# A Fourier mixing layer and a SiLU feed-forward on one core: preparation of the operands cut into smaller pieces and reordered

## The chip, the cores and the metric

The kernel runs on one core of a Trainium2 chip. A core has five engines that work side by side, each with a queue of its own: TensorE (PE; its weight loads are shown as PEld), VectorE (DVE), ScalarE (ACT), GpSimd (POOL) and SyncE (SP), which here only issues DMAs. The metric is the device time of one execution in microseconds, as the median of several runs; less is better. The kernel before takes 760.5 us (median of three, 759.12 to 760.71).

## What is computed

With x of 2048 tokens by 512 features:

```python
a = x_ln @ hid_re.T ;  b = x_ln @ hid_im.T          # x_ln = layernorm(x)
h = x + (seq_re @ a - seq_im @ b)                   # sequence DFT, 2048 x 2048
out = h + silu(layernorm(h) @ w1) @ w2              # w1 512 x 1792, w2 1792 x 512
```

All data are fp32. The layernorms have no gain or bias.

## The kernel before, in words

**Arithmetic.** Every fp32 operand of TensorE is kept as two rounded parts: `hi`, a copy rounded to the format fp32r that ACT makes (`ph`, `X`, `S`, `T..h`, `wah`, `wsh`), and `lo`, the remainder, which DVE makes by a subtraction (`pl`, `wal`, `wsl`). One product is three matmuls (`three`, lines 106 to 108): hi by hi, weight hi by lo, weight lo by hi. Each matmul is 128 x 128 by 128 x 512.

**Stages**, in the order of TensorE:
- *plain(0,0)*, the plain stage: the real sequence DFT of half of the output tokens, in 16 steps of 24 matmuls. A step is named (jj, k, tau): jj is one of four tiles of 512 rows of x, k one of its halves of 256 rows (each holds two pieces a of 128 rows), tau one of two blocks of output tokens. A step needs the normalised x of (jj, k) as weights (`X`, hi and lo) and a chunk of the DFT matrix (`raw`, split into `ph` and `pl`). Two steps, tau 0 and 1, use the same X.
- *fast(1,0)*, then mix(0), fast(0,1), fast(1,1) and mix(1). The fast stages do other parts of the sequence DFT with seven products instead of eight (Strassen's scheme in Winograd's form); they need sums and differences of the quarters of x (`S` 1 to 4 for each jj), which `sums_x` makes. A fast stage has 28 steps of 12 matmuls: three groups of four (products 1, 3, 2), and then products 5, 7, 6, 4 for each jj, whose DFT operands are differences that DVE makes first (line 326). mix is the hidden DFT with the residual.
- `norm_h(q, tau, start)` is the second layernorm, spread over the time from `start` on: mean (+0: DVE sums, then a reduction over partitions on GpSimd), center (+7 and +9: DVE, and squares on ACT), variance (+12), root (+28) and scaling (+42, +44).
- *up(0)*, down(0), up(1), down(1): the feed-forward. up runs seven products per p (p = 0 to 6), each of 6 matmuls, in the same scheme; `prep_w1` makes the weights: `wah`/`wal` are the split of w1's quarters, `s1` to `s4` their sums, `wsh`/`wsl` the split of these. After product 1, 6 and 5 ACT copies the accumulator out (`cp`, `cp`, `cq`); after 2, 5 and 4 DVE adds such a copy (line 558), and ACT applies SiLU (line 554). Product 3 accumulates onto the same bank after product 5, so it needs the copy `cq` to be done.

**What sets the order.** The author writes an order by hand. A clock counts planned time: `step(n, ...)` lets n matmuls take n x 0.2265 us, so a step of 24 is 5.44 us and one of 12 is 2.72. Every piece of work is an event with a planned time: a step's `before` list gives leads ahead of its start (`PREP_US` 8, `LOAD_US` 18), its `after` list delays after its end, and `at(t, f)` an absolute time. The events are sorted by that time, and on DVE, ACT and GpSimd the instructions of a later event are issued behind those of an earlier one. Planned times are thus only an order: an engine never waits for the clock, but each of these three queues is worked off in order, and an instruction that waits holds up all that is behind it. Within one event, and on TensorE and SP, a scheduler of the language chooses the order.

**Memory.** Nearly every operand lives in one of 51 slots of 4 KB per partition (the pool `pages`). A load waits until its slot is free. PSUM has four tiles of two banks.

**x's normalisation before.** `norm_x` (line 135) does it all in one event: statistics of each tile of 128 rows (lines 142 and 143), a reciprocal square root by three Newton iterations of three small DVE instructions each (`rsqrt`, lines 91 to 102), the normalised copy `xc` on ACT (line 150) and X's hi part (line 163); the remainders follow in a later event (`rest`, line 169). For jj = 1, 2, 3 all four tiles are in one event, 15 us ahead of the step (jj, 0, 0), and its remainders 11 us ahead. For jj = 0 the first two tiles are done singly at the very start, 128 rows each, and the other two 11 us ahead of (0, 1, 0). `sums_x(jj)` comes right after step (jj, 1, 0) for every jj, its remainders 3 us later.

Of the kernel before, what the change touches and what calls it, by code (L numbers as in the profile page):

```python
# [7 lines left out]
F32 = mybir.dt.float32  # L8
# [7 lines left out]
P = 128  # L16
# [21 lines left out]
def fnet_ffn_kernel(  # L38
# [52 lines left out]
    def rsqrt(v, t, r, q):  # L91
# [6 lines left out]
        for a, b in ((r, q), (q, r), (r, q)):  # L98
            nc.vector.tensor_tensor(t, a, a, op=ALU.mult)
            nc.vector.tensor_tensor(t, t, v, op=ALU.mult)  # L100
            nc.vector.scalar_tensor_tensor(b, t, 1.5, a, op0=ALU.add, op1=ALU.mult)
# [33 lines left out]
    def norm_x(jj, which):  # L135

        n = len(which)
        mv = small.tile([P, 4, 2], F32, name="mv1")
        w = small.tile([P, 5, 4], F32, name="rs1")
        for j, (k, a) in enumerate(which):  # L140
            st = small.tile([P, 6], F32, name="st1")
            nc.vector.bn_stats(st, xraw[jj, k][:, a, :])
            nc.vector.bn_aggr(mv[:, j, :], st)
# [3 lines left out]
        for j, (k, a) in enumerate(which):  # L147
            if (jj, k) not in xc:
                xc[jj, k] = page(f"xc{jj}{k}")
            nc.scalar.activation(  # L150
                xc[jj, k][:, a, :], xraw[jj, k][:, a, :], AF.Identity, bias=w[:, 4, j : j + 1], scale=r[:, j : j + 1]
            )
# [59 lines left out]
    def begin(key):  # L212

        t = raw[key] = page("raw")
        part[key] = page("ph", F32R), page("pl", F32R)
        src = seq[0, 0, 0].rearrange("p (a t) -> p a t", a=2)
        for a in range(2):
            load_x(0, 0, slice(a, a + 1))
            nc.sync.dma_start(t[:, a, :], src[:, a, :])

    def begin_norm(key, a):
        hi, lo = part[key]
        nc.scalar.activation(hi[:, a, :], raw[key][:, a, :], AF.Copy)
        late["x", a] = [(lo[:, a, :], raw[key][:, a, :], hi[:, a, :])] + norm_x(0, [(0, a)])
        if a == 1:
            raw.pop(key)

    def plain(c, q):

        for jj, k, tau in ((jj, k, tau) for jj in range(NJ) for k in range(2) for tau in range(2)):  # L230
            key = ("A", c, q, jj, k, tau)

            def mm(jj=jj, k=k, tau=tau, key=key):
                hi, lo = part.pop(key)
                for i in range(2):
                    if jj == 0 and k == 0:
                        acc[c, q, i, tau] = banks(f"c{c}{q}{i}{tau}")
                for a in range(2):
                    for i in range(2):
                        w = X[i, k, jj]  # L240
                        for m in range(2):
                            d = slice(m * P, (m + 1) * P)
                            three(acc[c, q, i, tau][:, m, :], w[:, 0, a, d], w[:, 1, a, d], hi[:, a, :], lo[:, a, :],
                                  jj == 0 and k == 0 and a == 0, jj == NJ - 1 and k == 1 and a == 1)

            before, after = [], []
            if (jj, k, tau) == (0, 0, 0):
                before = [(99.0, lambda key=key: begin(key))]
                for a in range(2):
                    before += [(98.0 - a, lambda a=a, key=key: begin_norm(key, a)),  # L250
                               (97.5 - a, lambda a=a: rest(late.pop(("x", a))))]
            else:
                before = [(LOAD_US, lambda jj=jj, k=k, tau=tau, key=key: load_seq(c, q, jj, k, tau, key)),
                          (PREP_US, lambda key=key: prep_raw(key))]
            if (jj, k, tau) == (0, 1, 0):
                before = [(40.0, lambda: load_x(0, 1)), (PREP_US + 3, lambda: early("x0", lambda: norm_x(0, [(1, 0), (1, 1)]))),
                          (PREP_US + 1, lambda: rest(late.pop("x0")))] + before
# [453 lines left out]
```

## Time and profile before

| | us |
|---|---|
| median of the runs | 760.5 |
| the profiled execution, its time | 761.24 |
| its span, first to last instruction | 759.3 |
| PE busy | 717.4 (94%) |
| DVE busy | 496.4 (65%) |
| ACT busy | 313.5 (41%) |
| POOL busy | 49.9 (7%) |

The mean granted clock of TensorE is 0.986. The program has 3036 matmuls of the kernel's own, and 15 that only warm the array up at the start (line 664). Matmuls are pipelined: a matmul's listed time (0.39 us) is longer than the distance between two starts, so progress is read from starts, and a busy PE is not a PE at its peak. A bracket behind a row, as in `[2.33 <-ACT X L163]`, is the idle time of that engine ahead of the row and what ended it. A name such as `ph` in a row stands for all buffers of that name.

### The profile page before, as it was taken

The page shows a single profiled execution, that of the slowest core. Times are in us where ns is not written, and L with a number is a line of the kernel's source. Part 1 is how long each engine was busy: PE and PEld are TensorE (multiplying, and loading weights), DVE is VectorE, ACT ScalarE, POOL GpSimd, SP SyncE. Part 2 cuts the span into 40 slices and gives each one's busy share as a digit, 9 for nine tenths or more (in the row PEclk, how much of TensorE's full clock was granted, in tenths as well). Part 3 has the DMA queues.
Part 4 walks back from the last instruction along what each step waited for, and adds up shares of the span by engine and source line. Part 5 has one row for each costly group of instructions (what it writes and reads, how often), then busy time and mean ns, then how long its engine had stood idle before and what let it go on. Part 6 is the DMA issues. An engine that isn't in the chain of part 4 may idle for free. (4 is left out here: it accounts for less than half of the span.)

```text
span 759.3 us, 8093 instructions
## 1 busy us (share of the span) xinstructions
PE 717.4 (94%) x3051; PEld 573.0 (75%) x3051; DVE 496.4 (65%) x672; ACT 313.5 (41%) x389; POOL 49.9 (7%) x48
## 2 busy tenths in 40 slices
PE   7699899999999999989999989999999989999997
PEld 4487688888888888868888866768778766778885
DVE  6586666694845899778986955437879844449002
ACT  3525455444223445144443435545432345457000
POOL 0000000000002210130000000002510000000000
PEclk9999999999999999999999999999999999999999
DMA  9322338555366658486952220232420411043003
GB/s 340 131 110 83 140 102 315 156 208 190 139 246 226 222 196 311 172 333 230 319 213 83 84 83 28 83 111 81 170 56 30 149 53 48 29 133 116 1 0 111
DMA packets 39592, 110.66 MB, mean 146 GB/s; under 512 B 4097, under 2 KB 7681, under 8 KB 39553
## 3 DMA queue, kind: packets, MB, share of 16 engines
q1 hardware_dynamic: 35968, 98.58, 37.1%
q0 software_dynamic: 3584, 11.56, 4.1%
q8 instruction: 24, 0.39, 0.2%
q14 instruction: 16, 0.12, 0.1%
HBM read 95.43 MB, written 14.70 MB: 145 GB/s over the span
## 5 line engine op out<-in xcount | busy, mean ns | idle before, releaser
L80 DVE TENSOR_TENSOR pl<-raw,ph 128x1024 fp32r<-128x1024 f32 x51 | 67.0, 1342 | 64.8 <-ACT ph L76 58.8
L106 PE MATMUL c<-ph,X 128*128 128x512 f32 x128 | 51.7, 411 | 14.5 <-ACT ph L76 9.9
L76 ACT ACTIVATE ph<-raw 128x1024 fp32r<-128x1024 f32 x51 | 51.2, 1050 | 21.2 <-PE y L107 12.0
L326 DVE TENSOR_TENSOR raw<-raw,raw 128x1024 f32<-128x1024 f32 x48 | 58.7, 1222 | 0.0
L107 PE MATMUL c<-pl,X 128*128 128x512 f32 x128 | 51.6, 404 | 0.6 <-DVE pl L80 0.5
L554 ACT ACTIVATE g<-g 128x512 f32<-128x512 f32 x42 | 26.5, 630 | 61.6 <-DVE g L558 61.6
L108 PE MATMUL c<-ph,X 128*128 128x512 f32 x128 | 51.0, 400 | 0.0
L106 PEld LDWEIGHTS c<-ph,X 128*128 128x128 f32 x128 | 24.5, 194 | 22.9 <-ACT ph L76 12.6
L629 DVE TENSOR_TENSOR ho<-o,ho 128x512 f32<-128x512 f32 x16 | 10.0, 688 | 47.5 <-PE o L108 47.3
L80 DVE TENSOR_TENSOR pl<-g,ph 128x1024 fp32r<-128x1024 f32 x28 | 34.0, 1238 | 5.4 <-ACT ph L76 5.4
L108 PE MATMUL m<-ph,X 128*128 128x512 f32 x96 | 37.4, 389 | 0.0
L107 PE MATMUL m<-pl,X 128*128 128x512 f32 x96 | 37.4, 389 | 0.0
L106 PE MATMUL m<-ph,X 128*128 128x512 f32 x96 | 37.3, 389 | 0.0
L558 DVE TENSOR_TENSOR g<-yx,cp 128x512 f32<-128x512 f32 x14 | 9.7, 692 | 32.4 <-PE yx L108 32.4
L107 PEld LDWEIGHTS c<-pl,X 128*128 128x128 f32 x128 | 25.0, 195 | 7.2 <-DVE pl L80 1.7
L108 PEld LDWEIGHTS c<-ph,X 128*128 128x128 f32 x128 | 25.0, 195 | 5.4 <-DVE X L169 0.2
L76 ACT ACTIVATE ph<-g 128x1024 fp32r<-128x1024 f32 x28 | 28.4, 1044 | 0.0
L558 DVE TENSOR_TENSOR g<-v,cq 128x512 f32<-128x512 f32 x14 | 9.7, 691 | 26.0 <-ACT cq L573 24.4
L528 DVE TENSOR_TENSOR wal<-w,wah 128x768 fp32r<-128x768 f32 x14 | 13.4, 957 | 20.3 <-ACT wah L523 20.3
L150 ACT ACTIVATE xc<-x,rs 128x512 f32<-128x512 f32 x16 | 11.9, 805 | 35.3 <-DVE rs L146 26.0
L459 ACT ACTIVATE sq<-hr 128x1024 f32<-128x1024 f32 x8 | 8.5, 1062 | 36.9 <-DVE hr L455 23.1
L436 POOL PARTITION_ALL_REDUCE m<-m x4 | 15.1, 3764 | 126.1 <-DVE g L558 75.8
(330 smaller groups left out, 1998.3 us busy)
## 6 DMA issues: line engine op xcount, KB each, us to landing
raw<-in_seq SPq DMA_DIRECT2D x99, 512.0 KB, 4.5
w<-in_ffn SPq DMA_DIRECT2D x28, 256.0 KB, 2.9
w<-in_ffn SPq DMA_DIRECT2D x14, 512.0 KB, 3.7
hid<-in_hid SPq DMA_DIRECT2D x8, 512.0 KB, 4.3
c<-cd SPq DMA_DIRECT2D x8, 512.0 KB, 4.3
h<-in_xT SPq DMA_DIRECT2D x8, 512.0 KB, 5.0
hd<-h POOLq DMA_DIRECT2D x8, 512.0 KB, 3.2
hr<-hd SPq DMA_DIRECT2D x8, 512.0 KB, 3.9
```

Of the source, the lines that this page charges most:

```text
L76: nc.scalar.activation(hi, src, AF.Copy, scale=sign)
L80: nc.vector.tensor_tensor(lo, src, hi, op=ALU.subtract)
L106: nc.tensor.matmul(acc, wh, mh, start=first, stop=False, skip_group_check=on)
L107: nc.tensor.matmul(acc, wh, ml, start=False, stop=False, skip_group_check=on)
L108: nc.tensor.matmul(acc, wl, mh, start=False, stop=last, skip_group_check=on)
L150: nc.scalar.activation(xc[jj, k][:, a, :], xraw[jj, k][:, a, :], AF.Identity, bias=w[:, 4, j : j + 1], scale=r[:, j : j + 1])
L326: nc.vector.tensor_tensor(o, a, b, op=ALU.subtract)
L436: nc.gpsimd.partition_all_reduce(t[:, 1, :], t[:, 0, :], channels=P, reduce_op=REDUCE_ADD)
L528: nc.vector.tensor_tensor(al[:, 1:, :], r[:, 1:, :], ah[:, 1:, :], op=ALU.subtract)
L554: nc.scalar.activation(g[q, f][:, tau, :], src, AF.Silu)
L558: nc.vector.tensor_tensor(d, src, other, op=ALU.add)
L629: nc.vector.tensor_tensor(t[:, tau, :], a[:, tau, :], t[:, tau, :], op=ALU.add)
```

## The change

Six things, each an edit of the event lists but for the first:
- In `rsqrt`, where the operand has one column, the first two instructions of an iteration become one (a x v x a, with v as a scalar per partition).
- `norm_x` is cut into `stats_x`, `roots_x` and `norm_x`. For jj = 1, 2, 3 the two halves k get statistics, normalised copies and remainders of their own, with one root in between. For jj = 2 and 3 they lie 19 and 16 us (statistics), 15 (root), 11 and 10 (copies), 8 and 5 us (remainders) ahead of the step (jj, 0, 0), for jj = 1 everything but the loads 5 us later; x is loaded 28 and 27 us ahead instead of 24. For the second half of jj = 0 statistics and root lie 9 us ahead of step (0, 1, 0), the copies 6 and the remainders 4.
- The first two steps are turned round: 24 matmuls with the first 128 rows of x for both blocks of tokens, then 24 with the second 128 rows. Both blocks' chunks of the DFT matrix are loaded and split by halves.
- `sums_x` of jj = 2 and 3 moves out of the plain stage into fast(1,0): 1 us and 8 us after its start, the remainders 4 us after each.
- norm_h(0,1) starts 8 us after the beginning of fast(1,1) instead of 1 us.
- In up, a weight's preparation is three events instead of two: the hi copy and the four sums 11 us ahead, the sums' hi copy and the first remainder 9.6, the sums' remainder 8.2 (before: all but the last at 10, the last at 8). SiLU after products 2, 5 and 4 becomes an event of its own, 1.5 us behind the add.

The diff's core:

```diff
@@ rsqrt
-            nc.vector.tensor_tensor(t, a, a, op=ALU.mult)
-            nc.vector.tensor_tensor(t, t, v, op=ALU.mult)
+            if a.shape[-1] == 1:
+                nc.vector.scalar_tensor_tensor(t, a, v, a, op0=ALU.mult, op1=ALU.mult)
+            else:
+                nc.vector.tensor_tensor(t, a, a, op=ALU.mult)
+                nc.vector.tensor_tensor(t, t, v, op=ALU.mult)
@@ x's normalisation
+    def stats_x(jj, which):
+        if jj not in stats:
+            stats[jj] = [], small.tile([P, 4, 2], F32, name="mv1"), small.tile([P, 5, 4], F32, name="rs1")
+        done, mv, _ = stats[jj]
+        for k, a in which:
             st = small.tile([P, 6], F32, name="st1")
             nc.vector.bn_stats(st, xraw[jj, k][:, a, :])
+            nc.vector.bn_aggr(mv[:, len(done), :], st)
+            done.append((k, a))
+    def roots_x(jj):
...
+        return {t: (w[:, 4, j : j + 1], r[:, j : j + 1]) for j, t in enumerate(done)}
+    def norm_x(jj, which, factors):
...
@@ plain
+        keys = [("A", c, q, 0, 0, tau) for tau in range(2)]
+        at(-99, lambda: begin(keys))
+        for a in range(2):
+            at(-98 + 4 * a, lambda a=a: begin_x(keys[0], a))
+            at(-97 + 4 * a, lambda a=a: rest(late.pop(("x", a))))
+            at(-96 + 4 * a, lambda a=a: rest(begin_half(keys[1], a)))
+            step(24, lambda a=a: [mul(0, 0, tau, [a], part[key]) for tau, key in enumerate(keys)])
+        at(-40, lambda: load_x(0, 1))
+        at(clock[0] - 9, lambda: (stats_x(0, [(1, 0), (1, 1)]), early("r0", lambda: roots_x(0))))
+        at(clock[0] - 6, lambda: early("x0", lambda: norm_x(0, [(1, 0), (1, 1)], late.pop("r0"))))
+        at(clock[0] - 4, lambda: rest(late.pop("x0")))
...
+            if k == 0 and tau == 0:
+                for k2, l1, l2, l3 in ((0, 19, 11, 8), (1, 16, 10, 5)):
+                    tiles = [(k2, 0), (k2, 1)]
+                    l1, l2, l3 = (l - 5 * (jj == 1) for l in (l1, l2, l3))
+                    before += [(28 - k2, lambda jj=jj, k=k2: load_x(jj, k)),
+                               (l1, lambda jj=jj, tiles=tiles: stats_x(jj, tiles)),
+                               (l2, lambda jj=jj, tiles=tiles, k=k2:
+                                early(("x", jj, k), lambda: norm_x(jj, tiles, late["r", jj]))),
+                               (l3, lambda jj=jj, k=k2: rest(late.pop(("x", jj, k))))]
+                before.append((15 - 5 * (jj == 1), lambda jj=jj: early(("r", jj), lambda: roots_x(jj))))
-            if k == 1 and tau == 0:
+            if k == 1 and tau == 0 and jj < 2:
                 after += [(0, lambda jj=jj: early(("s", jj), lambda: sums_x(jj))),
                           (3, lambda jj=jj: rest(late.pop(("s", jj))))]
...
+        for jj in range(2, NJ):
+            t = clock[0] + 1 + 7 * (jj - 2)
+            at(t, lambda jj=jj: early(("s", jj), lambda: sums_x(jj)))
+            at(t + 4, lambda jj=jj: rest(late.pop(("s", jj))))
@@ up
-        nc.vector.tensor_tensor(al[:, 1:, :], r[:, 1:, :], ah[:, 1:, :], op=ALU.subtract)
-        nc.scalar.activation(sh, t, AF.Copy)
-        late["w", q, p] = [(sl, t, sh)]
+        late["w", q, p] = [[(al[:, 1:, :], r[:, 1:, :], ah[:, 1:, :])], [(sl, t, sh)]]
...
         def add(f, tau, src, other):
-            d = g[q, f][:, tau, :]
-            nc.vector.tensor_tensor(d, src, other, op=ALU.add)
-            silu(f, tau, d)
+            nc.vector.tensor_tensor(g[q, f][:, tau, :], src, other, op=ALU.add)
...
-                before = [(LOAD_US, lambda p=p: load_w1(q, p)), (PREP_US + 2, lambda p=p: prep_w1(q, p)),
-                          (PREP_US, lambda p=p: rest(late.pop(("w", q, p))))]
-            step(6, lambda n=n, p=p: mm(n, p), before, [(0, lambda n=n, p=p: post(n, p))])
+                def sums(p=p):
+                    _, [(_, t, sh)] = late["w", q, p]
+                    nc.scalar.activation(sh, t, AF.Copy)
+                    rest(late["w", q, p][0])
+                before = [(LOAD_US, lambda p=p: load_w1(q, p)), (PREP_US + 3, lambda p=p: prep_w1(q, p)),
+                          (PREP_US + 1.6, sums), (PREP_US + 0.2, lambda p=p: rest(late.pop(("w", q, p))[1]))]
+            after = [(0, lambda n=n, p=p: post(n, p))]
+            if n in (2, 5, 4):
+                f, tau = {2: (2 * p, 0), 5: (2 * p + 1, 1), 4: (2 * p + 1, 0)}[n]
+                after.append((1.5, lambda f=f, tau=tau: silu(f, tau, g[q, f][:, tau, :])))
+            step(6, lambda n=n, p=p: mm(n, p), before, after)
@@ order of the stages
-    norm_h(0, 1, clock[0] + 1)
+    norm_h(0, 1, clock[0] + 8)
```

More of the change, by code (lines that the diff above doesn't have):

```diff
@@ new lines, in mul @@
+        def mul(jj, k, tau, tiles, parts):
+            hi, lo = parts
+            if jj == 0 and k == 0 and 0 in tiles:
+                for i in range(2):
+                    acc[c, q, i, tau] = banks(f"c{c}{q}{i}{tau}")
+            for a in tiles:
+                for i in range(2):
+                    w = X[i, k, jj]
+                    for m in range(2):
+                        d = slice(m * P, (m + 1) * P)
+                        three(acc[c, q, i, tau][:, m, :], w[:, 0, a, d], w[:, 1, a, d], hi[:, a, :], lo[:, a, :],
+                              jj == 0 and k == 0 and a == 0, jj == NJ - 1 and k == 1 and a == 1)
```

73 lines of the change are left out of this document (23 added, 50 removed).

## The prediction, made before the changed kernel was run

> **What bounds the kernel now.** I read the windows by stage first, cut at the stages' first matmuls (columns: window, length, then busy time and instruction count of PE, PEld, DVE, ACT, POOL, the granted clock, DMA share, GB/s).
>
> ```profile
> 8.09:114.83 106.74, 93.78 (x384) 73.91 (x385) 70.94 (x167) 49.26 (x70) 1.23 (x2) 0.95 0.40 146
> 114.83:190.99 76.16, 76.16 (x338) 63.06 (x337) 53.48 (x48) 35.97 (x39) 1.06 (x2) 1.00 0.60 211
> 310.66:392.93 82.27, 79.19 (x337) 63.97 (x336) 72.00 (x76) 36.58 (x39) 12.68 (x11) 0.98 0.74 272
> 436.22:516.75 80.53, 73.43 (x295) 54.68 (x294) 38.80 (x58) 38.38 (x60) 1.06 (x2) 0.98 0.22 75
> 516.75:596.26 79.51, 76.83 (x337) 62.90 (x336) 66.50 (x91) 35.04 (x37) 18.55 (x12) 1.00 0.25 78
> 596.26:677.45 81.19, 73.49 (x295) 54.59 (x294) 38.86 (x62) 36.46 (x59) 0.00 (x0) 0.98 0.25 81
> 677.45:753.64 76.19, 76.19 (x338) 63.06 (x336) 25.64 (x26) 19.62 (x22) 0.00 (x0) 1.00 0.17 54
> ```
>
> TensorE is the bound. The second row is a stage without a gap: its 336 matmuls (28 steps of 12) in 76.16 us are 0.2267 us each. At that pace the plain stage (first row, 384) would take 87.0 us; it takes 106.7, a loss of 19.7. The third row, fast(1,1), loses 6.1; the two up stages (294 matmuls, 66.65 us) lose 13.9 and 14.5; down(0) loses 3.3. Only those losses can be won, and the waits of PE name them (waiter, releaser: total us, times, longest):
>
> ```profile
> PE c L106 <- ACT ph L76: 9.9, 5, 6.0
> PE yx L106 <- ACT cq L573: 9.7, 10, 2.0
> PE c L106 <- ACT X L163: 4.5, 2, 2.3
> PE yx L106 <- DVE g L558: 1.7, 10, 0.2
> ```
>
> Three of the four rows are waits that the change is aimed at: both c rows lie in the plain stage, the cq row in the up stages. The fourth stays.
>
> **Plain stage, what costs now.** The stalls on PE's timeline (start, length, then in brackets the idle time before it):
>
> ```profile
> 13.51 0.50 PE L106 MATMUL c<-ph,X 128*128 128x512 f32 x1 [2.33 <-ACT X L163]
> 14.42 0.63 PE L106 MATMUL c<-ph,X 128*128 128x512 f32 x1
> 17.73 0.39 PE L108 MATMUL c<-ph,X 128*128 128x512 f32 x1
> 23.70 0.73 PE L106 MATMUL c<-ph,X 128*128 128x512 f32 x2
> 36.27 1.22 PE L106 MATMUL c<-ph,X 128*128 128x512 f32 x2 [6.03 <-ACT ph L76]
> 87.14 0.74 PE L106 MATMUL c<-ph,X 128*128 128x512 f32 x2 [2.82 <-ACT ph L76]
> ```
>
> From 14.42 to 17.73 nine matmuls start, eight intervals of 0.41 instead of 0.23: a slow clock after the 2.33 us gap, 1.5 us more. A wait of 2 us therefore costs its length, some 0.3 of refilling, and perhaps 1.5. The 2.82 us gap at 87.14 brought no such stretch, so the length alone does not decide.
>
> The Trainium skill (TensorE: Matmul & The Clock Gate, Part 1) has the clock fall after at least one idle window of about 3.4 us, and advises against idle gaps over some 3 us. The row at 13.51 contradicts it: 2.33 us was enough here. By the page, the 2.1 us gap that I leave below would cost no 1.5, and the total would come out 1.5 lower.
>
> **Part by part.** Prices, from groups of the first 116 us (busy, mean ns | idle):
>
> ```profile
> L80 DVE TENSOR_TENSOR pl<-raw,ph 128x1024 fp32r<-128x1024 f32 x18 | 21.8, 1224 | 30.6 <-ACT ph L76 24.6 <-DMA raw<-in_seq 6.0
> L76 ACT ACTIVATE ph<-raw 128x1024 fp32r<-128x1024 f32 x18 | 17.9, 1043 | 0.0
> L150 ACT ACTIVATE xc<-x,rs 128x512 f32<-128x512 f32 x16 | 11.9, 805 | 35.3 <-DVE rs L146 26.0 <-issue 9.3
> L142 DVE BATCH_NORM_STATS2 st<-x 128x6 f32<-128x512 f32 x16 | 10.5, 676 | 2.2 <-DMA x<-in_x 2.2
> L169 DVE TENSOR_TENSOR S<-s,S 128x512 fp32r<-128x512 f32 x16 | 10.0, 685 | 0.0
> L163 ACT ACTIVATE X<-xc 128x512 fp32r<-128x512 f32 x14 | 7.7, 615 | 0.0
> L100 DVE TENSOR_TENSOR rs<-rs 128x1 f32<-128x1 f32 x6 | 1.0, 160 | 0.2
> ```
>
> *The fused root.* Only the two one-column roots of the first tile lose three instructions each, 0.16 busy and about 0.2 with the gap between dependent ones: 0.6 us ahead of the first matmul: it starts at 7.5, not 8.09. The fused form (a per-partition scalar operand) has no row; between 0.16 us as its neighbours and twice that, I take 0.16 (at twice, 0.5 less is won).
>
> *Two blocks on the first tile.* Half 0 now feeds 24 matmuls (to 13.2) before half 1 is needed. Half 1 adds the second block's two ops in front (ACT hi and DVE lo, 0.6 each), then its own chain, 0.6 shorter: its first X is there at 13.1. The 13.51 gap and its slow stretch go. These 48 matmuls end at 18.6, where before the next step began at 23.70. The new load of the second block's halves delays the x half behind it by 256 KB; it is needed only at 8.9, so nothing.
>
> *What is late next* is X of x rows (0,1). DVE runs the second block's lo until 14.6, then two statistics, the unfused two-column root (13 small ops) until 18.5, ACT two xc and one X: PE starts at 20.75. Gap 2.1 us, with refill 2.5, and I charge the slow clock, 1.5.
>
> *Pieces.* Before, four tiles of statistics, root, four xc and four X ran as one block and the step's ph stood behind them in ACT's queue:
>
> ```profile
> 30.07 0.16 DVE L146 SCALAR_TENSOR_TENSOR rs<-mv,rs 128x4 f32<-128x4 f32 x1
> 30.27 2.92 ACT L150 ACTIVATE xc<-x,rs 128x512 f32<-128x512 f32 x4 [6.62 <-DVE rs L146]
> 33.10 2.17 ACT L163 ACTIVATE X<-xc 128x512 fp32r<-128x512 f32 x4
> 35.17 1.99 ACT L76 ACTIVATE ph<-raw 128x1024 fp32r<-128x1024 f32 x2
> ```
>
> Now ph of that step (1,0,0) is queued ahead of the xc. I laid the queues in the new order with the prices above (ends, us). DVE: X's remainders 22.1, first statistics 23.5, pl of (0,1,1) 24.7, second statistics 26.1, root 28.7, pl of (1,0,0) 29.8, four sums 32.2, X's remainders 33.4. ACT: ph of (0,1,1) 22.4, of (1,0,0) 23.4, two xc 30.3, X 31.0 and 31.5, S 33.6, second piece 36.2, ph of (1,0,1) 37.2. PE: (0,1,0) from 20.75, 24 matmuls and 0.3 for a late remainder, (0,1,1) from 26.5, ready for (1,0,0) at 31.95 (before: 36.27), when its X has been there since 31.0. The two later tiles go the same way. Left over are X's remainder behind the four sums (0.6), ph and pl of (1,0,1) behind S's and the second piece (0.4), pl of (1,1,0) behind the next statistics (0.9), (2,0,0) 1.0, (2,0,1) 0.7, (3,0,0) 0.8; with 0.2 at the very start and 4.0 above the new loss is 8.6 instead of 19.7. With the 0.6 of the start: **11.7 us** won. Bounds: 17 (all gone but the first gap), 5 (half of the old big gaps kept). x's earlier loads (28 against 24 us) run on SP far ahead of use and cost nothing while slots of the pool are free.
>
> *Sums of tiles 2 and 3 moved* behind the plain stage, into fast(1,0), which has no loss now.
>
> ```profile
> 103.34 0.69 DVE L176 TENSOR_TENSOR s<-xc,xc 128x512 f32<-128x512 f32 x1
> 116.17 3.89 ACT L76 ACTIVATE ph<-raw 128x1024 fp32r<-128x1024 f32 x4
> ```
>
> Per tile it is four sums, four S, four remainders: 2.5 us of DVE, 3.5 from first sum to last S, 2.5 of DVE. The second row shows that ACT comes back to ph only 1.3 us after fast(1,0) begins at 114.83, once C is copied out. From there I lay both queues: pl of the fourth step at +2.4, sums of tile 2 to +6.1, remainders to +11.7, sums of tile 3 from +12.8; ph of the seventh step stands behind their S until +17.35, its pl ends at +18.6, and PE wants it at +16.5 (six steps of 2.72, one matmul). **2.2 us lost.** Bounds: 0 (the queues had 1 us in hand twice) to 5.
>
> *norm_h(0,1) seven us later.* It touches fast(1,1):
>
> ```profile
> 319.68 4.40 DVE L80 TENSOR_TENSOR pl<-raw,ph 128x1024 fp32r<-128x1024 f32 x2
> 320.02 3.98 POOL L436 PARTITION_ALL_REDUCE m<-m  x1 [37.17 <-DMA raw<-in_seq]
> 325.41 1.06 ACT L459 ACTIVATE sq<-hr 128x1024 f32<-128x1024 f32 x1 [10.76 <-DVE hr L455]
> ```
>
> While GpSimd reduces, two pl take 4.4 us instead of 2.4, and ACT stands 10.8 us before the squares, with every ph of this stage behind them: that is the whole 6.1. Seven us later in the order DVE has worked off its backlog from the stage before, the mean starts at about 320.1 and three more ph/pl pairs precede center, so the steps up to 337 are covered. Then the variance (1.9 us on DVE), its reduction (another 2 of slowing) and, in ACT's queue, t5h ahead of the twelfth step's ph: pl is ready at 343.5, wanted at 340.85; with refill 3.1 is lost. POOL's stores of C come ahead of the reduction and gain time; what needs the normalised h (its loads, 40 us before up(0)) has over 20 us in hand. **3.0 us won**; bounds 6.1 and 0, below nothing if the root and the scalings, now deeper in the stage where DVE needs 2.3 of each 2.7 us, wait once more (-2).
>
> *Up stages.* One period, at T3's wait for the copy cq (PE's rows last: T7's final matmul, T3's first):
>
> ```profile
> 458.75 0.83 ACT L523 ACTIVATE wah<-w 128x768 fp32r<-128x768 f32 x1
> 460.95 1.06 ACT L529 ACTIVATE wsh<-ws 128x1024 fp32r<-128x1024 f32 x1 [1.36 <-DVE ws L527]
> 461.92 0.58 ACT L573 ACTIVATE cq<-yx 128x512 f32<-128x512 f32 x1
> 461.48 0.39 PE L108 MATMUL v<-T7h,wsl 128*128 128x512 f32 x1
> 462.55 0.50 PE L106 MATMUL yx<-T3h,wsh 128*128 128x512 f32 x1 [0.68 <-ACT cq L573]
> ```
>
> cq stands behind wsh, which waits 1.36 us for the fourth sum, which DVE does after wal, which waits for wah. The change puts wal behind the sums and wsh into a later piece: the order on ACT becomes wah, SiLU, wsh, cq, with the sums done under wah. In my layout cq ends 0.5 us before T7 does, so T3 waits no more: from start to start 1.07 instead of 0.23, 0.84, in four periods of each up stage. The first wait of each (2.0, the longest in the waits) shrinks by 1.4 and loses its slow stretch (1.5). That is 6.3 per stage, **12.6 us** in two. The SiLUs 1.5 us later delay only their own outputs, needed in down, 9 us or more on; the wait for the add (1.7 us) stays, and so do T5's and down's first. Bounds: 16 (the add's waits, 1.7 and as much refill, go too) and 0 (another order of the products on PE, which this kernel does not write out by hand, puts cq behind something else).
>
> **The sum.** 11.7 - 2.2 + 3.0 + 12.6 = 25.1. The profiled execution took 761.24 (span 759.3), so 736.1; it stands 0.7 above the median of 760.5.
>
> **Rivals.**
> 1. *Up keeps its wait* (PE's order shifts, or the SiLU ahead of wsh waits for its add and hands its lateness on to cq). For it: cq now has one more instruction ahead, and that add needs T4's end. Against: T4 ends four products before. 736.1 + 12.6 = 748.7.
> 2. *DVE stays late in the plain stage.* Its work there is only redistributed, and 70.9 busy of 106.7 us becomes some 61 of 95 (two tiles' sums gone). If every new piece still meets its step late, half of the gain is left: 736.1 + 5.9 = 742.0.
> 3. *All new waits miss.* No slow clock at the 2.1 us gap, none in fast(1,0) and fast(1,1): 736.1 - 1.5 - 2.2 - 3.1 = 729.3.
> 4. *Slower: slots of the pool.* That slots run out shows in SP's own waits, with the landing time of a load below (KB each, us to land):
>
> ```profile
> SPq L133 <- DVE s L177: 18.8, 1, 18.8
> raw<-in_seq SPq DMA_DIRECT2D x99, 512.0 KB, 4.5
> ```
>
> x of tile 3 waited 18.8 us for a sum to free its slot. Those sums now come for tiles 2 and 3 only in fast(1,0). If a load for its first steps holds a slot of xc(2), it starts at +6.1, lands 4.5 later, and ph and pl (2.2) follow: 12.8 us of PE. The same for xc(3): 25.6, with two slow stretches 28.6, and 736.1 + 28.6 = 764.7. It decides only if both happen. Against: a tile's sums take six slots and give three at once, so two tiles not yet summed leave more free, not fewer.
>
> **Chances and range.** Forecast (732 to 741) 0.50; rival 3 0.13; rival 2 0.14; rival 1 0.16; rival 4 0.07. 0.2%, 1.5 us, is about what a measurement here can tell from no change. All but rival 4 are faster: 0.92, 0.01 for no change, 0.07 slower. The range 727 to 749 takes in the first four.
>
> **What would show it.** Right: PE's first matmul near 7.5, no wait at half 1, one gap of 2 us before the third step, no gap over 1 us later in the plain stage, its end near 103; a wait of some 2 us at the seventh step of fast(1,0); fast(1,1) near 79 us; no PE wait for cq beyond each up stage's first, each stage near 74. Wrong: cq still in PE's waits, ph still behind xc in ACT's queue before tiles 1 to 3, SP's loads named as PE's releasers, or new waits of DVE's pl in the second half of fast(1,1).

## The result, and the profile after

The changed kernel takes 732.07 us (median of four runs, 730.76 to 732.91), the kernel before 760.61 on the same chip (759.12 to 760.88): a ratio of 0.9627 [0.9608, 0.9646]. The profiled execution took 732.91 (span 730.9), 28.3 us less than the one before, at a mean granted clock of 0.995 instead of 0.986. The forecast was 736.1, its range 727 to 749.

The windows by stage of the kernel after, cut at the stages' first matmuls (window, length, then PE, PEld, DVE, ACT, POOL, clock, DMA share, GB/s): plain, fast(1,0), fast(1,1), up(0), down(0), up(1).

```profile
7.90:102.03 94.13, 90.27 (x385) 71.17 (x386) 62.78 (x151) 45.46 (x63) 1.24 (x2) 1.00 0.46 169
102.03:181.46 79.43, 77.03 (x338) 62.91 (x336) 61.81 (x62) 40.51 (x46) 1.07 (x2) 1.00 0.57 201
301.14:379.13 77.99, 76.78 (x337) 62.99 (x336) 69.04 (x75) 35.69 (x38) 12.99 (x11) 1.00 0.78 286
422.65:497.32 74.67, 71.50 (x296) 55.14 (x294) 39.67 (x59) 39.29 (x60) 1.21 (x3) 0.98 0.25 88
497.32:576.77 79.45, 76.93 (x337) 62.76 (x336) 67.11 (x93) 34.03 (x36) 19.41 (x12) 1.00 0.24 77
576.77:649.11 72.34, 70.54 (x295) 53.87 (x295) 38.95 (x60) 38.17 (x60) 0.00 (x0) 1.00 0.29 95
```

The forecast's rows of the kernel before were cut up to 1.5 us ahead of the stages' first matmuls. Cut at them, its plain, down(0) and up(1) are:

```profile
8.09:115.05 106.96, 94.00 (x384) 74.09 (x385) 71.16 (x167) 49.41 (x70) 1.23 (x2) 0.95 0.40 146
517.21:597.71 80.50, 76.99 (x338) 62.74 (x336) 67.53 (x93) 35.03 (x37) 18.52 (x12) 1.00 0.24 75
597.71:677.92 80.21, 73.34 (x295) 54.75 (x295) 37.41 (x59) 36.93 (x60) 0.00 (x0) 0.98 0.26 84
```

Set against the same matmuls at 0.2267 us each, the losses are as follows (the first row is time until PE starts):

| | loss before | loss after | won | forecast |
|---|---|---|---|---|
| start, until the first matmul | 8.1 | 7.9 | 0.2 | 0.6 |
| plain | 19.9 | 7.1 | 12.8 | 11.1 |
| fast(1,0) | 0 | 3.3 | -3.3 | -2.2 |
| fast(1,1) | 6.1 | 1.8 | 4.3 | 3.0 |
| up(0) | 13.9 | 8.0 | 5.9 | 6.3 |
| down(0) | 4.3 | 3.3 | 1.0 | 0 |
| up(1) | 13.6 | 5.7 | 7.9 | 6.3 |
| sum | | | 28.8 | 25.1 |

The other stages are as long as before, and the end behind the last matmul is 0.4 us longer. What TensorE still waits for is in its waits after (waiter, releaser: total us, times, longest):

```profile
PE c L109 <- ACT X L176: 4.0, 2, 2.0
PE yx L109 <- ACT cq L597: 3.5, 2, 2.5
...
PE m L110 <- DVE pl L80: 1.5, 2, 0.8
...
PE c L110 <- DVE pl L80: 1.3, 3, 0.4
PE m L109 <- ACT ph L76: 1.2, 2, 0.8
...
PE m L111 <- DVE S L182: 0.8, 1, 0.8
...
PE c L109 <- ACT ph L76: 0.5, 2, 0.3
```

The 9.9 us of c waiting for ph are gone but for 0.5. The cq wait fell from ten times to two, 9.7 to 3.5 us: only each up stage's first is left. The waits of yx for the add (1.7 before) are gone too. The m rows are the fast stages; PE's timeline after shows where these waits lie:

```profile
21.51 0.50 PE L109 MATMUL c<-ph,X 128*128 128x512 f32 x1 [2.02 <-ACT X L176]
...
119.31 0.50 PE L109 MATMUL m<-ph,S 128*128 128x512 f32 x1 [0.80 <-ACT ph L76]
120.57 0.50 PE L110 MATMUL m<-pl,S 128*128 128x512 f32 x1 [0.76 <-DVE pl L80]
124.89 0.50 PE L111 MATMUL m<-ph,S 128*128 128x512 f32 x1 [0.84 <-DVE S L182]
...
331.94 0.50 PE L109 MATMUL m<-ph,X 128*128 128x512 f32 x1 [0.45 <-ACT ph L76]
333.20 0.50 PE L110 MATMUL m<-pl,X 128*128 128x512 f32 x1 [0.76 <-DVE pl L80]
...
436.01 0.50 PE L109 MATMUL yx<-T3h,wsh 128*128 128x512 f32 x1 [2.45 <-ACT cq L597]
588.83 0.50 PE L109 MATMUL yx<-T3h,wsh 128*128 128x512 f32 x1 [1.03 <-ACT cq L597]
```

The first is the gap that the forecast left standing before the third step (2.1 us there, 2.02 here). The next two are the seventh step of fast(1,0), 17.3 and 18.5 us after its start. The fourth was not foreseen. The first cq wait of up(0) is 2.45 us, longer than any before; that of up(1) is 1.03.

### The profile page after: what moved, and what is told of

The parts are those of the page before. It is cut to its first block, busy times and chain, and to the rows that moved or that the text cites. A ratio compares the mean times of both kernels' runs of the same rounds, so it can differ in the third digit from the quotient of the medians.

```text
span 730.9 us, 8090 instructions
## 1 busy us (share of the span) xinstructions
PE 707.3 (97%) x3051; PEld 568.6 (78%) x3051; DVE 494.2 (68%) x667; ACT 315.6 (43%) x390; POOL 51.2 (7%) x48
## 4 chain that ended last, share of the span: by engine, by line
PE 42%; DVE 7%; issue 2%; ACT 2%; DMA 1%; POOL 0%; DVEq 0%; POOLq 0%; ACTq 0%
PE yx L109 5%; PE yx L111 4%; PE yx L110 4%; PE o L109 4%; PE o L111 4%; PE o L110 4%; PE m L110 2%; PE m L111 2%; PE m L109 2%; PE y L110 2%; PE y L109 2%; PE y L111 2%; PE v L109 2%; PE v L110 2%; PE v L111 2%
## 5 line engine op out<-in xcount | busy, mean ns | idle before, releaser
L80 DVE TENSOR_TENSOR pl<-raw,ph 128x1024 fp32r<-128x1024 f32 x50 | 63.0, 1284 | 57.4 <-ACT ph L76 57.4
L109 PE MATMUL c<-ph,X 128*128 128x512 f32 x128 | 49.6, 395 | 4.6 <-ACT X L176 4.0
L111 PE MATMUL c<-ph,X 128*128 128x512 f32 x128 | 49.5, 391 | 0.0
L109 PEld LDWEIGHTS c<-ph,X 128*128 128x128 f32 x128 | 24.0, 188 | 11.8 <-ACT X L176 5.6
L111 PEld LDWEIGHTS c<-ph,X 128*128 128x128 f32 x128 | 24.0, 188 | 5.7 <-DVE X L182 0.9
L165 ACT ACTIVATE xc<-x,rs 128x512 f32<-128x512 f32 x16 | 12.3, 810 | 32.3 <-DVE rs L156 23.9
L583 DVE TENSOR_TENSOR g<-v,cp 128x512 f32<-128x512 f32 x14 | 9.7, 691 | 23.8 <-PE v L111 23.8
L110 PEld LDWEIGHTS m<-pl,X 128*128 128x128 f32 x96 | 18.0, 188 | 4.8 <-DVE pl L80 1.1
L109 PEld LDWEIGHTS m<-ph,X 128*128 128x128 f32 x96 | 18.0, 188 | 4.5 <-ACT ph L76 0.8
```

What stands on the lines that cost most here:

```text
L80: nc.vector.tensor_tensor(lo, src, hi, op=ALU.subtract)
L109: nc.tensor.matmul(acc, wh, mh, start=first, stop=False, skip_group_check=on)
L110: nc.tensor.matmul(acc, wh, ml, start=False, stop=False, skip_group_check=on)
L111: nc.tensor.matmul(acc, wl, mh, start=False, stop=last, skip_group_check=on)
L165: nc.scalar.activation(xc[jj, k][:, a, :], xraw[jj, k][:, a, :], AF.Identity, bias=bias, scale=scale)
L583: nc.vector.tensor_tensor(g[q, f][:, tau, :], src, other, op=ALU.add)
```

## The experiments

My theory was the forecast's: order in the queues of ACT and DVE made the waits, each edit removes the wait it touches, and the edits add up. The rivals were that one part does it all, that TensorE's order of the products (which a scheduler chooses) does it in the up stages, and, for the single pieces, that another lead or another cover does as well. Ratios are to the kernel before on the same chip.

### One part alone, on the kernel before

**All the edits of x** (fused root, shared first tile, pieces, sums moved), with norm_h and up as before:

```diff
@@ rsqrt, begin, stats_x / roots_x / norm_x, plain
+ (all of the change's lines in these functions)
@@ up, order of the stages
  (as before)
```

> The kernel before with the changes to x's normalisation alone (fused root, shared first tile, pieces, the sums of tiles 2 and 3 moved behind the plain stage); norm_h and up as before. My theory, that the three parts of the change act in stages of their own and add up: the traces of before and after have the plain stage 12.6 us shorter, the start 0.2 earlier and fast(1,0) 3.3 longer, so 9.5 us less, 751; fast(1,1) and up keep their losses of 6.1, 13.9 and 14.5. Rival, that an earlier x part moves the DVE and ACT queues of later stages as well: more than 2 us off that sum, with fast(1,1) or up changed.

Measured: 750.46 us, 0.9864 [0.9841, 0.9888], against 761.03 before. Its windows for plain and fast(1,0):

```profile
7.99:101.99 94.00, 90.97 (x384) 72.64 (x385) 62.77 (x151) 45.35 (x63) 1.23 (x2) 0.98 0.46 169
101.99:181.43 79.44, 77.07 (x337) 62.91 (x336) 61.81 (x62) 40.46 (x46) 1.06 (x2) 1.00 0.57 202
```

The lengths are those of the changed kernel within 0.2 us; its fast(1,1) still loses 6.1 and its up stages 12.3 and 13.6. The 1.6 us that up(0) lost more in the profile before are a slow stretch that this execution did not have there (clock 1.00 instead of 0.98). So x's part is worth 10.6 us, and no wait of a later stage goes with it. What the fused root and the earlier loads of x give by themselves was not run.

**norm_h(0,1) seven us later, alone:**

```diff
-    norm_h(0, 1, clock[0] + 1)
+    norm_h(0, 1, clock[0] + 8)
```

> The kernel before with norm_h(0,1) started 8 us instead of 1 us after the beginning of fast(1,1), nothing else. My theory: the loss of fast(1,1) falls from 6.1 to 1.8, so 4.3 us less, 756.3, with the wait left at the twelfth step, where t5h stands ahead of ph in ACT's queue. The prediction's own sum would have 3.0. Rival, that the gain in fast(1,1) comes from the earlier start of everything before it: no change, 760.6.

Measured: 756.47 us, 0.9944 [0.9926, 0.9963]; 4.6 us. The stage is as long as in the changed kernel (77.99):

```profile
312.36:390.34 77.98, 76.77 (x338) 62.98 (x337) 69.05 (x76) 35.64 (x38) 12.97 (x11) 1.00 0.78 285
```

**The weights in three events, alone**; the add still calls SiLU:

```diff
@@ up
-                before = [(LOAD_US, ...), (PREP_US + 2, lambda p=p: prep_w1(q, p)),
-                          (PREP_US, lambda p=p: rest(late.pop(("w", q, p))))]
+                before = [(LOAD_US, ...), (PREP_US + 3, lambda p=p: prep_w1(q, p)),
+                          (PREP_US + 1.6, sums), (PREP_US + 0.2, lambda p=p: rest(late.pop(("w", q, p))[1]))]
```

> The kernel before with the weights' preparation of up in three events, the SiLUs left right behind their adds. TensorE's own order of products stays as before. My theory, that cq is late only because wsh waits for the sum behind wal: the four waits of 0.84 and the first long one with its slow stretch go in each up stage, 12 to 13 us less in all, 748; the short waits for the add (0.43 with the refill, four per stage) stay. Rival, that the waits went because TensorE's products come in another order in the changed kernel (product 4 whole behind product 2): the waits for cq stay and the time is within 2 us of before.

Measured: 747.19 us, 0.9818 [0.9795, 0.9842]; 13.8 us. Windows of the two up stages, and then PE's waits there:

```profile
438.05:511.34 73.29, 70.35 (x295) 53.90 (x294) 39.48 (x58) 37.17 (x59) 1.08 (x3) 1.00 0.26 91
590.96:664.26 73.30, 70.52 (x296) 53.94 (x296) 37.86 (x59) 36.49 (x60) 0.00 (x0) 1.00 0.28 92
```

```profile
PE yx L106 <- ACT cq L571: 1.4, 2, 0.7
PE yx L106 <- DVE g L556: 1.7, 10, 0.2
```

The products stand in PE's order as before, and still eight of ten cq waits are gone: it was ACT's queue, not PE's order. The period of seven products fell from 11.1 to 10.08 us. The add's ten short waits stay, as the forecast had it for the whole change.

**SiLU apart from the add, alone:**

```diff
@@ up
         def add(f, tau, src, other):
-            d = g[q, f][:, tau, :]
-            nc.vector.tensor_tensor(d, src, other, op=ALU.add)
-            silu(f, tau, d)
+            nc.vector.tensor_tensor(g[q, f][:, tau, :], src, other, op=ALU.add)
...
+            if n in (2, 5, 4):
+                f, tau = {2: (2 * p, 0), 5: (2 * p + 1, 1), 4: (2 * p + 1, 0)}[n]
+                after.append((1.5, lambda f=f, tau=tau: silu(f, tau, g[q, f][:, tau, :])))
```

> The kernel before with the SiLUs 1.5 us behind their adds, the weights' preparation in two events as before. The order of products on TensorE changes by itself. My theory: cq still stands behind wsh and wsh behind wal, so T3's wait of about 0.7 stays in every period; the short waits for the add go with the new order of products (0.43 by 8 to 10, some 4 us less), and the first SiLU's table load, now in front of the weights, gives back about 1: 757. Rival, that product order is what cured the cq waits: 12 us less or more, 748.

Measured: 760.93 us, 1.0003 [0.9985, 1.002]: nothing, which I had not expected. Its cq wait, and ACT's timeline in one period:

```profile
PE yx L106 <- ACT cq L571: 14.8, 10, 4.0
```

```profile
464.32 1.06 ACT L529 ACTIVATE wsh<-ws 128x1024 fp32r<-128x1024 f32 x1 [1.36 <-DVE ws L527]
465.29 0.58 ACT L571 ACTIVATE cq<-yx 128x512 f32<-128x512 f32 x1
```

With SiLU apart, TensorE's order of the products changes (product 2 now comes ahead of 4) and the waits for the add vanish. But wsh waits 1.36 us for the fourth sum exactly as before, cq stands behind it, and behind each stage's first the cq waits grow from 0.7 to 1.0 us. The period stays at 11.1: the loop over ACT and DVE (wah, wal, fourth sum, wsh, cq) sets it, and what one wait gives up the next one takes. Only with the weights' order mended does the SiLU edit show, as a period of 9.85 instead of 10.08 in the changed kernel.

The three working parts give 10.6 + 4.6 + 13.8 = 29.0 us, the whole 28.5: they add up.

### One part taken out or altered, on the kernel after

**No shared first tile**, but the pieces and the fused root kept:

```diff
-            at(-98 + 4 * a, lambda a=a: begin_x(keys[0], a))
-            at(-97 + 4 * a, lambda a=a: rest(late.pop(("x", a))))
-            at(-96 + 4 * a, lambda a=a: rest(begin_half(keys[1], a)))
-            step(24, lambda a=a: [mul(0, 0, tau, [a], part[key]) for tau, key in enumerate(keys)])
+            at(-98 + 2 * a, lambda a=a: begin_x(keys[0], a))
+            at(-97 + 2 * a, lambda a=a: rest(late.pop(("x", a))))
+            at(-94 + a, lambda a=a: rest(begin_half(keys[1], a)))
+        for tau, key in enumerate(keys):
+            step(24, lambda tau=tau, key=key: mul(0, 0, tau, (0, 1), part[key]))
```

> The changed kernel with its first two steps as before: 24 matmuls of the first block of tokens over both halves of x's first tile, then 24 of the second block; the second block's halves are split behind the first's, nothing else is different. My theory, that what is late next (the X of x rows (0,1), ready at 21.4) swallows most of what the sharing saves: PE waits some 2.3 us at half 1 again, perhaps with a slow stretch of 1.5, and in return not at the third step, so 0.3 to 1.5 us more, 732.4 to 733.6. Rival, that the sharing is worth the whole gap and slow stretch it removes: 4 us more, 736.

Measured: 732.31 us, 0.9628 [0.9606, 0.965], against 0.9627 with it. The gap only moves (PE's timeline):

```profile
12.99 0.50 PE L109 MATMUL c<-ph,X 128*128 128x512 f32 x1 [1.99 <-ACT X L176]
```

It is back at the second half of the first tile, 1.99 us, and the one before the third step is gone. One gap of 2 us remains either way, since x's first tiles are prepared one behind the other; sharing buys matmuls to put ahead of the second half and pays with two more operations in front of the third.

**The sums of tiles 2 and 3 back in the plain stage:**

```diff
-            if k == 1 and tau == 0 and jj < 2:
+            if k == 1 and tau == 0:
...
-        for jj in range(2, NJ):
-            t = clock[0] + 1 + 7 * (jj - 2)
-            at(t, lambda jj=jj: early(("s", jj), lambda: sums_x(jj)))
-            at(t + 4, lambda jj=jj: rest(late.pop(("s", jj))))
```

> The changed kernel with the sums of tiles 2 and 3 back in the plain stage, behind the steps (2,1,0) and (3,1,0) as before. My theory, that the 3.3 us which fast(1,0) now loses come from these sums in ACT's and DVE's queues: they go, and tile 3's pieces then lose about what tile 2's lose beside the sums of tile 1 (1.7), so 1.6 us less than the changed kernel, 730.5. Rival, that the pieces of tile 3 are on time only because these sums were moved away: the plain stage loses more than 3.3, 732 to 735.

Measured: 730.21 us, 0.9604 [0.958, 0.9627]. Fast(1,0) is again without a gap, and the plain stage, from 7.93 to 102.95, is 95.02 us, against 94.13:

```profile
102.95:179.11 76.16, 76.16 (x337) 63.09 (x336) 53.43 (x48) 35.82 (x38) 1.06 (x2) 1.00 0.55 203
```

**Only the sums of tile 3 moved:**

```diff
-            if k == 1 and tau == 0 and jj < 2:
+            if k == 1 and tau == 0 and jj < 3:
...
-        for jj in range(2, NJ):
-            t = clock[0] + 1 + 7 * (jj - 2)
+        for jj in range(3, NJ):
+            t = clock[0] + 1 + 7 * (jj - 3)
```

> The changed kernel with the sums of tile 2 back in the plain stage and only those of tile 3 behind it, 1 and 5 us after the start of fast(1,0). My theory: fast(1,0) loses nothing, since one tile's sums are done ahead of the seventh step; the plain stage loses 1.7 more as with both back; 730.5. Rival, that the copies of C which ACT makes at the start of fast(1,0) make even one tile's sums late: fast(1,0) keeps 2 or more.

Measured: 729.60 us, 0.9592 [0.9569, 0.9616]. Plain loses 8.0 us and fast(1,0) nothing. In both kernels plain and fast(1,0) together are 2.4 us shorter than in the changed kernel (171.2 in each against 173.6). The intervals of the whole times overlap with that of the changed kernel, so the loss in fast(1,0) is shown by the windows, and in the time only likely.

**The first period's SiLUs not put off:**

```diff
-                after.append((1.5, lambda f=f, tau=tau: silu(f, tau, g[q, f][:, tau, :])))
+                after.append((0 if p == 0 else 1.5, lambda f=f, tau=tau: silu(f, tau, g[q, f][:, tau, :])))
```

The suspicion came from ACT's timeline of the changed kernel in the first period of up(0):

```profile
431.25 0.60 ACT L595 ACTIVATE cp<-yx 128x512 f32<-128x512 f32 x1 [6.44 <-PE yx L111]
431.87 1.28 ACT L580 ACT_TABLE_LOAD   x1
433.16 0.63 ACT L580 ACTIVATE g<-g 128x512 f32<-128x512 f32 x1
433.70 0.83 ACT L551 ACTIVATE wah<-w 128x768 fp32r<-128x768 f32 x1
434.43 1.04 ACT L619 ACTIVATE wsh<-ws 128x1024 fp32r<-128x1024 f32 x1
435.38 0.58 ACT L597 ACTIVATE cq<-yx 128x512 f32<-128x512 f32 x1
```

The load of SiLU's table stands directly ahead of the first SiLU in the queue. In the kernel before it ran at 438.85, and ACT then stood idle for 3.7 us until the first SiLU could start; 1.5 us later in the order it is behind cp, and the next weights and cq stand behind it.

> The changed kernel with the SiLUs of the first p of each up stage right behind their adds again (the others stay 1.5 us behind). My theory, that the first wait for cq in up(0), 2.45 us, is long because the table load of 1.28 us for the first SiLU now stands just ahead of the weights' copy: it goes back to where ACT is idle, the wait falls to 0.7 and the slow stretch of 1.5 behind it goes, up(0) loses 5.3 instead of 8.0; 729.3. Rival, that the wait is set by the weights' chain alone: no change, 732.

Measured: 728.34 us, 0.958 [0.9554, 0.9605]. The first row is the window of up(0), 3.3 us shorter than in the changed kernel; the fence after it is PE's row of the timeline for the same wait, 0.69 instead of 2.45, and without the slow stretch that followed there (from 437.3 to 440.8):

```profile
422.42:493.78 71.36, 69.99 (x295) 53.95 (x294) 39.61 (x58) 39.15 (x61) 1.06 (x2) 1.00 0.26 91
```

```profile
434.25 0.50 PE L109 MATMUL yx<-T3h,wsh 128*128 128x512 f32 x1 [0.69 <-ACT cq L597]
```

Not all of the 3.3 us is the table load's. The profiles of no_share and sums_plain have the same order in up(0) and the same wait of 2.4 us, but no slow stretch behind it, and their up(0) takes 73.35 and 73.36 us. So some 2.0 us are the place of the load, and 1.3 the slow stretch, which an execution has or has not.

**The halves joined again**: for jj = 1, 2, 3 one event for the statistics, one for the copies and one for the remainders of all four tiles, at the new leads:

```diff
-                for k2, l1, l2, l3 in ((0, 19, 11, 8), (1, 16, 10, 5)):
-                    tiles = [(k2, 0), (k2, 1)]
...
+                every = [(k2, a) for k2 in range(2) for a in range(2)]
+                l1, l2, l3 = (l - 5 * (jj == 1) for l in (19, 11, 8))
```

> The changed kernel with x's tiles 1, 2 and 3 prepared as one block again: statistics of all four tiles of 128 rows in one event at the first half's lead (19 us, 14 for tile 1), one root, the four copies in one event (11, 6), the four remainders in one (8, 3). The leads are those of the change, only the cut by halves is gone. My theory, that what removed the 6 us gap is the step's ph standing ahead of the copies in ACT's queue, and the earlier statistics, not the cut: X's first piece comes two copies (1.5 us) later and the four remainders stand in one row, 0.5 to 2 us more than the changed kernel, 733 to 734. Rival, that the cut itself matters, since DVE and ACT are tied up in one row as before: the gaps ahead of tiles 1 to 3 come back in part, 4 us more or above, 736.

Measured: 731.54 us, 0.9623 [0.9587, 0.9659]: the cut into halves is worth nothing that this measurement can tell. In the profile the plain stage with the halves joined is even 1.0 us shorter, 93.15 against 94.13. ACT's timeline shows why:

```profile
21.80 1.99 ACT L76 ACTIVATE ph<-raw 128x1024 fp32r<-128x1024 f32 x2
...
29.05 2.94 ACT L165 ACTIVATE xc<-x,rs 128x512 f32<-128x512 f32 x4 [5.26 <-DVE rs L156]
...
36.06 2.95 ACT L76 ACTIVATE ph<-raw 128x1024 fp32r<-128x1024 f32 x3
```

All four xc are one block again, but the ph of the step (1,0,0) is in the row above it, at 21.80, instead of behind it at 35.17 as before the change. The order, that is the leads, did it; which of the leads (loads, statistics, copies, remainders) was not separated. Joining and no sharing at once were not tried.

**norm_h(0,1) another 3 us later:**

```diff
-    norm_h(0, 1, clock[0] + 8)
+    norm_h(0, 1, clock[0] + 11)
```

> The changed kernel with norm_h(0,1) started 11 us after the beginning of fast(1,1) instead of 8. My theory, that the 1.8 us which fast(1,1) still loses come from the variance on DVE standing ahead of the first difference, so that t5h and the twelfth step's ph behind it in ACT's queue are late: the variance now comes behind both, the wait goes, 730.3. Rival, that the work only moves: GpSimd's second reduction and the root now fall where DVE needs 2.3 of each 2.7 us, and as much is lost there, 732.

Measured: 733.99 us, 0.9659 [0.963, 0.9687]; fast(1,1) loses 2.4 instead of 1.8. GpSimd's second reduction now falls on t5l (timeline), and PE waits for that (waits):

```profile
332.14 4.07 POOL L464 PARTITION_ALL_REDUCE v<-v  x1 [15.40 <-DVE v L463]
333.04 3.26 DVE L80 TENSOR_TENSOR t5l<-raw,t5h 128x1024 fp32r<-128x1024 f32 x1
```

```profile
PE m L110 <- DVE t5l L80: 1.5, 1, 1.5
```

**Sums back in plain and the first SiLUs not put off**, the two mends together:

```diff
-            if k == 1 and tau == 0 and jj < 2:
+            if k == 1 and tau == 0:
...  (the loop over jj 2 and 3 behind plain is gone)
-                after.append((1.5, ...))
+                after.append((0 if p == 0 else 1.5, ...))
```

> The changed kernel with the two undone parts that each gained alone: all of sums_x back in the plain stage, and the first p's SiLUs right behind their adds. Theory, that they act in stages of their own and add up: 1.9 and 3.7 us less, 726.5. Rival, that part of the two gains was the luck of the slow clock: 728.3, no better than the second alone.

Measured: 727.46 us, 0.9578 [0.9549, 0.9607], the fastest kernel of this study; its interval lies wholly below that of the changed kernel. Windows of plain, fast(1,0) and up(0):

```profile
7.92:102.93 95.01, 90.89 (x385) 71.03 (x385) 71.14 (x165) 49.91 (x71) 1.23 (x2) 1.00 0.47 173
102.93:179.09 76.16, 76.16 (x338) 63.08 (x336) 53.44 (x49) 35.83 (x38) 1.06 (x2) 1.00 0.56 203
420.25:491.61 71.36, 69.99 (x296) 53.98 (x294) 39.66 (x59) 39.11 (x60) 1.55 (x3) 1.00 0.26 93
```

Plain costs 0.9 us more than in the changed kernel, fast(1,0) 3.3 less, up(0) 3.3 less (1.3 of them the slow stretch).

**The same with norm_h(0,1) at + 11:**

```diff
-    norm_h(0, 1, clock[0] + 8)
+    norm_h(0, 1, clock[0] + 11)
```

> The kernel of the run before this one with norm_h(0,1) started 11 us after the beginning of fast(1,1) as well. Theory: 1.8 less again, 724.7. Rival, as for that part alone: no change, 726.5.

Measured: 728.30 us, 0.9582 [0.9547, 0.9617]: no gain. In the profiled execution fast(1,1) loses 4.0 us: the wait for t5l of norm11, 1.54 us, and a slow stretch behind it, which norm11's own execution (2.4) did not have.

## Why the prediction was right, and where it was not

The total was right (732.07 in a range of 727 to 749, 4.0 below the forecast), because the three large terms were read off the right waits. That it is as near as 4.0 is partly luck: errors of both signs stand in the sum, as the table shows, and the 1.5 us charged for a slow clock in the plain stage and the gain counted for the shared first tile were wrong in kind. By its own steps:

- *The fused root*: too large. The fused form was the unknown, and DVE's groups by shape in the first 13 us of the changed kernel give its price (busy, mean ns of one | idle):

```profile
L100 DVE SCALAR_TENSOR_TENSOR rs<-rs 128x1 f32<-128x1 f32 x6 | 1.3, 219 | 0.2
L104 DVE SCALAR_TENSOR_TENSOR rs<-rs 128x1 f32<-128x1 f32 x6 | 1.0, 160 | 0.2
```

  0.219 us, between the 0.16 that I took and its double. From the first statistics to the root's last instruction it is 2.92 us instead of 3.25, so a root gains 0.33, not 0.6, and x's first statistics began 0.14 later. PE started 0.2 earlier, not 0.6.
- *Two blocks on the first tile*: right that the gap at 13.51 goes, and that one of 2.1 us comes at the third step. Wrong to count that as part of the gain: without sharing the same gap stands in the old place and the time is the same. The old gap cost nothing either. In up_weights, whose plain stage is that of the kernel before, no slow stretch followed it, and the second step started 1.7 us earlier (16.27 instead of 17.96), but the third only 0.1 (23.59 instead of 23.70) and the fourth 0.1 (36.13 instead of 36.27): the next operands were late anyway.
- *What is late next*: gap right (2.1 against 2.02). The slow clock charged for it, 1.5, was the mis-sized term, nearly all of the difference in plain (8.6 forecast, 7.1 measured). It did not come in this execution, but where it came it cost nothing: silu0 and norm11, which are the changed kernel up to there, had it, and their plain stage takes 94.05 and 93.98 us, against 94.13. The tenth step, (2,0,1), starts at 62.45, 62.43 and 62.47, so what ACT and DVE have prepared sets that moment, and a slow TensorE ahead of it only shortens later waits.
- *Pieces*: the gain is right, and right too is its reason as laid out in the queues, ph of (1,0,0) ahead of the xc. What the forecast did not separate is that the order alone gives it, not the cut.
- *Sums moved*: sign and place right (the seventh step, waiting for ph and pl), the size too small, 3.3 instead of 2.2. The layout stopped at that step; 4 us later PE waits 0.84 for a remainder of S, which costs a further 1.1 with its refill. What the move saves in the plain stage, which the forecast counted within the pieces, is only 0.9 us: 95.01 with the two tiles' sums there, 94.13 without.
- *norm_h later*: 4.3 won instead of 3.0. The twelfth step's wait came where it was put (30.8 us after the stage's start; forecast 30.2), but as 0.45 and 0.76 instead of 2.7 us. I charged the second reduction with slowing DVE in front of that pl, and there was none: DVE stood idle for 2.07 us until ACT had made the ph, and the pl took 1.23. norm11 shows how near that was, for 3 us later a slowed operation is on the path.
- *Up stages*: the mechanism is confirmed (eight of ten cq waits gone, with the products in the same order), total 13.8 against 12.6. The forecast's 14.5 for up(1) was misread: its row began 1.45 us early, in down(0), and up(1) lost 13.6. Two sizes were off. The first wait of up(0) did not shrink by 1.4 but grew to 2.45 and kept its slow stretch, because "the SiLUs 1.5 us later delay only their own outputs" forgot the table load that goes with the first. And the add's waits, said to stay, went, since the SiLU edit lets TensorE's order change; this and the better period in both stages more than paid for it.
- *Rival 1* is refuted by the waits (two cq waits left, not ten), *rival 2* by the plain stage (7.1, not 14.5), *rival 4* by the waits: no load is among PE's releasers. *Rival 3*, all new waits miss, at 729.3, did not happen as described: of its three waits the slow clock missed (and would have cost nothing there), one came at somewhat more than half its size and one came larger.

## What to carry to other kernels

Where engines work off their queues in order, first look for the instruction that stands waiting in front of the one TensorE needs, and move it: the order gave nearly all of the gain here; cutting the work smaller and sharing a first tile, each taken out by itself, changed nothing that could be measured. An edit that relieves one wait of a loop shows no gain while another wait of the same loop still sets the period (SiLU apart: 0 alone). A gap of TensorE costs nothing where what comes behind it is late anyway, as at the first tile here. And moving the first use of an activation function moves its table load with it, so the first period must be looked at by itself.

## What the runs showed of the hardware that was not expected

**Slow stretches behind short gaps.** The gap of 2.0 us at 21.5, the same in nine kernels' profiles, was followed in five of them by matmuls some 0.43 us apart, and in four by none. The gap of 2.8 us at 87 in the old plain stage brought such a stretch in three of four profiles, the 2.45 us gap in up(0) in four of six, and once a wait of 1.54 us was enough, and once two of 0.8 us one behind the other (no_share, fast(1,0)). The granted clock settles what decides. Windows of silu0, which had the stretch, and then of the changed kernel, which had not:

```profile
18.20:21.61 3.41, 1.41 (x7) 0.83 (x6) 2.13 (x8) 2.27 (x4) 0.00 (x0) 1.00 1.06 398
21.61:25.02 3.41, 3.41 (x8) 2.74 (x9) 3.41 (x7) 2.29 (x3) 0.00 (x0) 0.50 1.03 411
17.51:20.92 3.41, 1.98 (x9) 1.31 (x7) 2.59 (x10) 1.62 (x3) 0.00 (x0) 1.00 1.05 395
20.92:24.33 3.41, 2.82 (x12) 2.27 (x13) 2.84 (x7) 2.96 (x4) 0.00 (x0) 1.00 1.03 406
```

The clock falls to 0.5 for 3.41 us (behind the 6 us gap for twice that), and within each of the fourteen profiles all times at which it changes lie whole multiples of 3.41 us apart. So each execution has a grid of 3.41 us windows, whose place differs from execution to execution. In silu0 the gap fell within one window, which left PE busy for 1.41 us; in the changed kernel a border at 20.92 cut it, and neither window was idle for more than 1.43. Over all profiles, from the kernel's first matmul to its last, all 26 windows at full clock in which PE was idle for 1.9 us or more were followed by one at half the clock, and none of those under 1.55; from 1.55 to 1.80 us it was two of sixteen. The Trainium skill (TensorE: Matmul & The Clock Gate, Part 1) asks for an idle window of some 3.4 us; in these profiles 1.9 us of idle time within one was enough.

What a stretch costs depends on what is late behind it. At 87 in the old plain stage it was 1.5 us (106.96 without, 108.45 with it in up_weights), in up(0) 1.3, and in the new plain stage behind the gap at 21.5 nothing.

**The table load.** 1.28 us, in ACT's queue directly ahead of the first SiLU; in its new place it cost some 2.0 us of TensorE in up(0), and 3.3 with the slow stretch. The Trainium skill (ScalarE: Activation LUTs, What ACT_TABLE_LOAD costs) gives 1283 ns, which the trace confirms, and a drain of some 1.4 us beside it, of which the trace shows nothing: cp ends at 431.85 and SiLU starts at 433.16.

**DVE beside GpSimd's reduction.** One 128x1024 remainder takes 1.22 us by itself, and t5l took 3.26 beside the reduction, a factor of 2.7. In the profile before, two took 4.40. In the changed kernel, beside the reduction from 328.87 to 332.94, an operation that overlapped only its first microsecond and one that overlapped only its last took 1.22 and 1.23, so not all of a reduction slows DVE.
